# Attention scores on chip laid out by blocks of 32 queries first, and their mirrored copies in longer pieces

## The chip, the core and the metric

The kernel runs on one core of a Trainium2 chip. The core has five engines that work side by side, each with its own in-order stream of instructions: TensorE (PE; its weight loads are a row of their own, PEld), VectorE (DVE), ScalarE (ACT), GpSimd (POOL) and SyncE (SP), which here only issues DMAs. Sixteen DMA engines move data between the main memory (HBM) and the on-chip memory (SBUF); TensorE writes its products to PSUM. The metric is the device time of one execution in microseconds (us). Lower is better.

## What is computed

Two stages. The first is a gated attention unit without softmax: for each of 8 batches the scores of all pairs of 2496 positions, a squared ReLU, a product with `v`, and a gate `u`. The second sends each of the 19968 rows through one of 8 small networks, chosen by a hash of its token.

```python
scores = scale * np.matmul(z, z.transpose(0, 2, 1))     # z: 8 x 2496 x 64
attn = np.maximum(scores, 0.0) ** 2
out = np.matmul(attn, v)                                # v: 8 x 2496 x 256
x = (u * out).reshape(B * S, D)
...
expert_idx = token_ids * 2654435761 % 8
for e in range(8):
    mask = expert_idx == e
    out[mask] = np.maximum(x[mask] @ w1[e], 0.0) @ w2[e]   # 256 -> 1024 -> 256
```

All data is 32-bit floating point. Since queries and keys are both `z`, the scores of a batch are a symmetric matrix.

## The kernel before

**Tiling of the attention.** The 2496 positions of a batch are two halves of 1248. A query group `g` (0 to 4) takes the same 256 positions of both halves (the last group 224), a key step `s` (0 to 4) likewise. So a batch has 25 steps of (g, s), in the order `STEPS`; all 8 batches make 200. A tile `a` of one step holds 512 keys by 512 queries: 128 partitions, two tiles `j` of 128 keys, key half `h`, 8 blocks `m` of 32 queries (7 in the last group), query half `q`, and 32 queries `r` in a block. Before the change `a` is ordered `[j, h, m, q, r]` along a partition.

**Scores and their mirror.** Steps with `s >= g` are computed by `score`: four products on TensorE into PSUM (tag `mm`, four buffers), a ReLU by ScalarE for each (L244), then squares: on ScalarE (L250, L252), and for the step with `s == g` one half on VectorE (L248). When `s > g`, `mirror` transposes the tile on VectorE in 32 x 32 blocks (L274), and `keep` stores it to HBM through SP's queue in four DMAs (L283), or in seven for the last group of keys in the last batch (L287). Steps with `s < g` are not computed: `recall` reads the mirrored tile back by a DMA that ScalarE issues (L291). So 15 of 25 steps are computed, 10 are stored and read back: 80 tiles in all. The tiles `a` have four buffers, the mirrors two.

**One step.** `sums` makes four combinations `t` of the quarters of `a` on VectorE (L263 to L266); `attend` then makes seven products in place of eight (a scheme of Strassen's kind) of two matmuls each (L312) into the four PSUM tiles `acc`. The trace counts each 32-bit matmul as two MATMUL records, so a step has 28. Products 1, 2 and 3 read quarters of `a` as their moving operand, the others read `t`. After the last step of a group, `join` copies and adds the seven products (L323 to L331) and so frees the banks of `acc` for the next group; its second instruction is L325.

**What sets the order.** The order in each engine's stream is the order of the program text (`tc.manual_schedule()`). In loop pass `i` it is: `sums` for step `i + 2` (with its `score` ahead of it), `recall` for step `i + 3`, `keep` for the mirror made in the pass before, loads and transposes of the next batch's `z` (`load_z` L160, `turn_z` L173, `copy_z` L178), `attend` for step `i`, `join` if it ends a group, `mirror` for step `i + 2`, loads and sums of `v`. After these come the work on finished groups (`gate`, `put` L352, `fetch` L360 and L208, `multiply` L377, the scatter `sort` on GpSimd), the routing `places` during batch 0, and the preparation of the expert weights (`prepare`, L656 to L672). SP issues nearly all loads and stores in this order and waits in it for whatever each DMA needs; so does VectorE.

The second stage (L886 on) begins when the last group has been joined. It is run by the same kind of products (L928, L959, L982, L993) and reads weights and rows by DMA.

Of the kernel before, what the change touches and what calls it, by code (L numbers as in the profile page):

```python
# [10 lines left out]
F32 = mybir.dt.float32  # L11
# [13 lines left out]
def kernel(  # L25
# [10 lines left out]
    nc = tc.nc  # L36
# [4 lines left out]
    E, _, F = moe_w1.shape  # L41
# [3 lines left out]
    P = 128  # L45
    L = 32
# [18 lines left out]
    W = 256  # L65
# [10 lines left out]
    QB = P // L  # L76

    def in_turn(b, g):
        return (b, g) != (B - 1, NG - 1)
# [17 lines left out]
    def pool(name, bufs, **kw):  # L97
# [9 lines left out]
    mpool, zpool = (closing["z and mirrors"].enter_context(tc.tile_pool(name=name, bufs=2, side="right")) for name in ("mpool", "zpool"))  # L107
    vpool, apool, opool, xpool = (
        attention.enter_context(tc.tile_pool(name=name, bufs=bufs))
        for name, bufs in (("vpool", 6), ("apool", 3), ("opool", 2), ("xpool", 1)))  # L110

    def blocks(g):
        return min(W, HS - g * W) // L

    mirrored = {(b, g, s): nc.dram_tensor(f"scores_{b}_{g}_{s}", (2 * W, blocks(s) * 2 * L), F32)
                for b in range(B) for s in range(NG) for g in range(s)}


# [24 lines left out]
    def keys(s, j):  # L145
        return P if (s, j) != (NT - 1, 1) else KL

    def queries(g):
        return min(W, HS - g * W)
# [61 lines left out]
    def flat(ps):  # L211
        return ps[:].rearrange("p t q c -> p (t q c)")

    def score(b, g, s):

        w, nb = queries(g), blocks(g)
        a = apool.tile([P, 2, 2, W // L, 2, L], F32, name="a", bufs=4)
        made = []  # L220
        for j in range(2):
            for h in range(2):
                z_h = zT[b][ts(h, K), :]
                q_h = z_h[:, 0:S].rearrange("k (q c) -> k q c", q=2)[:, :, ds(g * W, w)]
                ps = mm_ps.tile([P, 2, 2, P], F32, name="s_ps", tag="mm")
                if w == W:
                    to, at = ps.rearrange("p t q c -> p q t c"), q_h.rearrange("k q (t c) -> k q t c", t=2)
                else:
                    to, at = flat(ps)[:, 0:2 * w].rearrange("p (q c) -> p q c", q=2), q_h
                nc.tensor.matmul(to, z_h[:, ds(h * HS + s * W + j * P, P)], at, start=True, stop=True)  # L230
                made.append((j, h, ps))
        for j, h, ps in made:

            if w == W:
                parts = ((a[:, j, h].rearrange("p (i t) q r -> p (t q) i r", t=2), ps[:].rearrange("p t q (i r) -> p (t q) i r", r=L)),)
            else:
                at = flat(ps)[:, 0:2 * w].rearrange("p (q m r) -> p q m r", q=2, r=L)
                if in_turn(b, g):
                    parts = [(a[:, j, h].rearrange("p (i t) q r -> p t q i r", t=2)[:, t, :, 0:keys(g, t) // L],
                              at[:, :, ds(t * QB, keys(g, t) // L)]) for t in range(2)]  # L240
                else:
                    parts = ((a[:, j, h, 0:nb].rearrange("p m q r -> p q m r"), at),)
            for to, at in parts:
                nc.scalar.activation(to, at, AF.Relu, scale=1.0 / S)  # L244
            if h:
                o = a[:, j].rearrange("p h m q r -> p h (m q r)")[:, :, 0:2 * w]
                if j and s == g:
                    nc.vector.tensor_mul(o, o, o)  # L248
                elif j:
                    nc.scalar.activation(o, o, AF.Square)  # L250
        o = a[:, 0].rearrange("p h m q r -> p h (m q r)")[:, :, 0:2 * w]
        nc.scalar.activation(o, o, AF.Square)  # L252
        return a

    def halves(a, g, h, q):
        return a[:, :, h, 0:blocks(g), q]

    def sums(g, a):

        t = apool.tile([P, 4, 2, W], F32, name="t")  # L260
        y11, y12, y21, y22 = (halves(a, g, h, q) for h in range(2) for q in range(2))
        t1, t2, t3, t4 = (t[:, i, :, 0:queries(g)].rearrange("p j (m r) -> p j m r", r=L) for i in range(4))
        nc.vector.tensor_sub(t1, y12, y11)  # L263
        nc.vector.tensor_sub(t3, y22, y12)  # L264
        nc.vector.tensor_sub(t2, y22, t1)  # L265
        nc.vector.tensor_sub(t4, t2, y21)  # L266
        return a, t

    def mirror(a):

        m = mpool.tile([P, 2 * W // L, 2, 2, L], F32, name="mirror")
        for j in range(2):
            for h in range(2):
                nc.vector.transpose(m[:, :, j, h].rearrange("p (n i) k -> p i n k", i=QB),  # L274
                                    a[:, j, h].rearrange("p (i t) q r -> p i (t q) r", t=2))
        return m

    def keep(b, g, s, m):
        to = mirrored[b, g, s].rearrange("(m r) e -> r m e", r=L)
        for i in range(QB):  # L280
            if in_turn(b, s):
                n = 2 * L * len(range(2 * i, min(2 * i + 2, blocks(s))))
                nc.sync.dma_start(out=to[:, :, ds(i * 4 * L, n)], in_=m[ts(i, L)].rearrange("p n j h k -> p n (j h k)")[:, :, 0:n])  # L283
            else:
                for j in range(2):
                    if j * QB + i < blocks(s):
                        nc.sync.dma_start(out=to[:, :, ts(j * QB + i, 2 * L)], in_=m[ts(i, L), :, j].rearrange("p n h k -> p n (h k)"))  # L287

    def recall(b, g, s):
        a = apool.tile([P, 2, 2, W // L, 2, L], F32, name="a", bufs=4)  # L290
        nc.scalar.dma_start(  # L291
            out=a[:].rearrange("p j h m q k -> p (j h) (m q k)")[:, :, 0:blocks(g) * 2 * L],
            in_=mirrored[b, s, g].rearrange("(n p) e -> p n e", p=P))
        return a


# [2 lines left out]
    def attend(b, g, s, at, acc, first, last):  # L299
        w = queries(g)  # L300
        a, t = at
        vs, c = v_sb[b, s], vc_sb[b, s]
        x11, x12, x21, x22 = (vs[:, h, :, ts(i, P)] for i in range(2) for h in range(2))
        s1, s2, s4 = (c[:, i] for i in range(3))
        y11, y12, y21, y22 = (halves(a, g, h, q) for h in range(2) for q in range(2))
        t1, t2, t3, t4 = (t[:, i, :, 0:w] for i in range(4))
        for i, (m, x, y) in enumerate(((1, x11, y11), (2, x12, y21), (5, s1, t1), (3, s4, y22), (6, s2, t2), (7, x21, t3), (4, x22, t4))):
            k, half = BANK[m]
            for j in range(2):
                n = keys(s, j)  # L310

                nc.tensor.matmul(acc[k][:, half, 0:w], x[0:n, j, :], y[0:n, j], start=(first and j == 0 and half == 0),  # L312
                                 stop=(last and j == 1), skip_group_check=True)
# [446 lines left out]
    def recall_early(i):  # L760
        if i < len(steps) and steps[i][2] < steps[i][1]:
            scores[i] = recall(*steps[i])

    def prepare_scores(i):
        if i < len(steps):
            b, g, s = steps[i]
            if s >= g and i >= AHEAD:
                scores[i] = score(b, g, s)
            ready[i] = sums(g, scores[i])
            return scores.pop(i)  # L770
# [6 lines left out]
    def prepare_mirror(i, a):  # L777
        if i < len(steps) and steps[i][2] > steps[i][1]:
            mirrors.append((*steps[i], mirror(a)))


    for i in range(AHEAD):
        scores[i] = score(*steps[i])
# [5 lines left out]
    for i, (b, g, s) in enumerate(steps):  # L789
        pos = i % NT  # L790
        to_keep, mirrors = mirrors, []
        a = prepare_scores(i + AHEAD)
        recall_early(i + AHEAD + 1)
        for m in to_keep:
            keep(*m)
# [58 lines left out]
        for part, after in enumerate((0, 4, 5, 7)):  # L854
            k, due = divmod(i - PREP - after, PERIOD)
# [170 lines left out]
    for i in range(NBIG + 1):  # L1026
        parts = {}
# [55 lines left out]
```

## Time and profile before

| | |
|---|---|
| median of 3 runs | 2508.42 us (2508.22 to 2512.26) |
| the profiled execution | 2508.14 us, its span 2506.4 us |
| ACT busy | 724.2 us, 29% |
| DMA packets | 583400 (284236 under 512 B, 525213 under 2 KB) |
| DMA queue of SP (q1) | 363.19 MB, 53.9% of 16 engines' span |
| DMA queue of ScalarE (q10) | 97.86 MB, 12.1% |
| store of a mirrored tile, 276 DMAs of 256 KB | median 5.0 us from issue to landing |
| read-back, 48 of 1024 KB and 32 of 896 KB | median 5.8 and 7.4 us |

The span is the time from the first to the last instruction of the program. A busy time is the time in which an engine had an instruction running. "Landing" is when a DMA's completion was signalled. A wait is idle time of an engine, put down to what ended it; the name behind `<-` is the engine, tile and line, or the DMA. The attention takes the first 1470 us of the span.

### The profile page before, as it was taken

How to read it: one execution, taken by the hardware profiler on the slowest of the kernel's cores; microseconds unless marked ns; L12 is line 12 of the kernel's file. 1: busy time of each engine (PE TensorE's matmuls, PEld its weight loads, DVE VectorE, ACT ScalarE, POOL GpSimd, SP SyncE). 2: the span in 40 equal slices, each digit the busy share in tenths (PEclk: the TensorE clock that was granted, in tenths of full speed). 3: DMA queues.
4: the chain of work that ended last, by engine and by line, in shares of the span. 5: the costliest groups of instructions: out<-in, count | busy, mean ns of one | idle time of the engine just before them, and what ended most of it. 6: DMA issues, size and time to landing. Idle time of an engine off the chain costs nothing.

```text
span 2506.4 us, 37323 instructions
## 1 busy us (share of the span) xinstructions
PE 2474.0 (99%) x13751; PEld 2110.9 (84%) x13751; DVE 1715.3 (68%) x3346; ACT 724.2 (29%) x1259; POOL 547.2 (22%) x532
## 2 busy tenths in 40 slices
PE   8999999999999999999999999999999999999998
PEld 6787786787787787787787889999999999999998
DVE  7799758768768778777677656655665565556554
ACT  4314313314324224223233112222222222222221
POOL 0000243233313331332233211111111111121212
PEclk9999999999999999999999999999999999999999
DMA  8766798798788798897897886767685767667672
GB/s 148 181 177 163 212 275 239 192 274 223 222 238 223 207 254 209 234 256 187 244 250 198 237 259 211 275 215 218 202 260 189 261 194 253 210 227 234 212 247 75
DMA packets 583400, 550.67 MB, mean 220 GB/s; under 512 B 284236, under 2 KB 525213, under 8 KB 571184
## 3 DMA queue, kind: packets, MB, share of 16 engines
q1 hardware_dynamic: 492720, 363.19, 53.9%
q10 hardware_dynamic: 63168, 97.86, 12.1%
q0 software_dynamic: 27328, 87.23, 9.8%
q8 instruction: 108, 1.77, 0.3%
q14 instruction: 76, 0.62, 0.1%
HBM read 371.36 MB, written 173.24 MB: 217 GB/s over the span
## 4 chain that ended last, share of the span: by engine, by line
PE 91%; DMA 4%; DVE 3%; issue 1%; ACT 0%; SPq 0%; POOL 0%; ACTq 0%; POOLq 0%; DVEq 0%
PE acc L312 42%; PE o_ps L959 17%; PE h_ps L928 17%; PE s_ps L230 9%; PE h_ps L982 3%; PE o_ps L993 3%; DMA a<-scores 2%; DMA u_sb<-in_u_dram 1%; DMA zn<-in_z_dram 0%; DMA scores<-mirror 0%; DVE t L263 0%; DVE t L264 0%; DVE x_row L377 0%; DVE t L265 0%; DVE t L266 0%
## 5 line engine op out<-in xcount | busy, mean ns | idle before, releaser
L244 ACT ACTIVATE a<-s_ps 128x512 f32<-128x512 f32 (+2 forms) x508 | 248.4, 578 | 751.8 <-PE s_ps L230 690.0
L312 PEld LDWEIGHTS acc<-a,v_sb 128*128 128x128 f32 (+1 forms) x1600 | 295.2, 191 | 128.7 <-issue 45.5
L312 PE MATMUL acc<-t,vc 128*128 128x256 f32 (+3 forms) x1600 | 403.1, 374 | 0.0
L312 PE MATMUL acc<-a,v_sb 128*128 128x256 f32 (+3 forms) x1600 | 385.8, 384 | 7.8 <-DVE o L325 7.7
L312 PE MATMUL acc<-t,v_sb 128*128 128x256 f32 (+3 forms) x1600 | 369.7, 373 | 0.0
L399 POOL DMA_INDIRECT x_slots<-x_row,row x160 | 185.9, 1162 | 819.6 <-DVE x_row L377 667.5
L312 PEld LDWEIGHTS acc<-t,vc 128*128 128x128 f32 (+1 forms) x1600 | 304.0, 190 | 34.5
L312 PEld LDWEIGHTS acc<-t,v_sb 128*128 128x128 f32 (+1 forms) x1600 | 303.4, 190 | 33.6
L263 DVE TENSOR_TENSOR t<-a 128x512 f32<-128x512 f32 (+1 forms) x200 | 134.2, 671 | 234.2 <-ACT a L252 164.6
L928 PE MATMUL h_ps<-xs,w 128*128 128x256 f32 (+1 forms) x1248 | 288.5, 361 | 0.0
L959 PEld LDWEIGHTS o_ps<-w,h 128*128 128x128 f32 x2272 | 275.8, 192 | 7.8 <-DVE ro L892 1.1
L880 POOL DMA_INDIRECT out_dram<-o_sb,idx x142 | 143.5, 1011 | 629.7 <-issue 406.5
L959 PE MATMUL o_ps<-w,h 128*128 128x128 f32 x2272 | 279.3, 275 | 0.6 <-DVE ro L892 0.6
L230 PE MATMUL s_ps<-zT 64*128 64x512 f32 (+1 forms) x960 | 244.7, 619 | 15.2 <-DVE zT L173 8.3
L935 ACT ACTIVATE h<-h 128x512 f32<-128x512 f32 (+1 forms) x234 | 138.5, 592 | 355.6 <-DVE h L898 143.5
L928 PEld LDWEIGHTS h_ps<-xs,w 128*128 128x128 f32 x1248 | 208.6, 191 | 16.5
L928 PE MATMUL h_ps<-xT,w 128*128 128x256 f32 (+1 forms) x936 | 215.0, 362 | 2.9 <-DVE h L898 2.9
L959 PEld LDWEIGHTS o_ps<-w,hs 128*128 128x128 f32 x1704 | 206.9, 192 | 4.9
L959 PE MATMUL o_ps<-w,hs 128*128 128x128 f32 x1704 | 209.3, 275 | 0.0
L274 DVE STREAM_TRANSPOSE mirror<-a 128x512 f32<-128x512 f32 x320 | 198.3, 676 | 5.4 <-DMA scores<-mirror 5.4
L312 PE MATMUL acc<-a,vc 128*128 128x256 f32 (+3 forms) x800 | 201.1, 373 | 0.0
L626 POOL DMA_INDIRECT slot_tokens<-token,addr x160 | 171.1, 1069 | 65.7 <-issue 48.4
(176 smaller groups left out, 2631.9 us busy)
## 6 DMA issues: line engine op xcount, KB each, us to landing
w<-w_blocks SPq DMA_DIRECT2D x78, 1792.0 KB, 11.0
scores<-mirror SPq DMA_DIRECT2D x276, 256.0 KB, 5.0
a<-scores ACTq DMA_DIRECT2D x48, 1024.0 KB, 5.8
a<-scores ACTq DMA_DIRECT2D x32, 896.0 KB, 7.4
w_blocks<-w POOLq DMA_DIRECT2D x16, 1792.0 KB, 7.6
w1s<-in_moe_w_dram SPq DMA_DIRECT2D x21, 1024.0 KB, 9.6
w2s<-in_moe_w_dram SPq DMA_DIRECT2D x21, 1024.0 KB, 15.6
u_sb<-in_u_dram SPq DMA_DIRECT2D x72, 256.0 KB, 5.4
```

What stands on the lines that cost most here:

```text
L230: nc.tensor.matmul(to, z_h[:, ds(h * HS + s * W + j * P, P)], at, start=True, stop=True)
L244: nc.scalar.activation(to, at, AF.Relu, scale=1.0 / S)
L263: nc.vector.tensor_sub(t1, y12, y11)
L274: nc.vector.transpose(m[:, :, j, h].rearrange("p (n i) k -> p i n k", i=QB), a[:, j, h].rearrange("p (i t) q r -> p i (t q) r", t=2))
L312: nc.tensor.matmul(acc[k][:, half, 0:w], x[0:n, j, :], y[0:n, j], start=(first and j == 0 and half == 0), stop=(last and j == 1), skip_gro ...
L399: st = nc.gpsimd.indirect_dma_start(out=x_dram[:, :], out_offset=bass.IndirectOffsetOnAxis(ap=row[0:m, c:c + 1], axis=0), in_=x_sb[0:m, q, ...
L626: st = nc.gpsimd.indirect_dma_start(out=slot_dram[:, None], out_offset=bass.IndirectOffsetOnAxis(ap=addr[0:n, to:to + 1], axis=0), in_=tok ...
L880: st = nc.gpsimd.indirect_dma_start(out=out[:], out_offset=bass.IndirectOffsetOnAxis(ap=idx[:, col:col + 1], axis=0), in_=o, in_offset=Non ...
L928: nc.tensor.matmul(ps[:, r], w1[j][:, k, ts(f + r, P)], y, start=first and r == 0, stop=True, skip_group_check=True)
L935: lambda o, i, k, ps=None: nc.scalar.activation(o, o if ps is None else ps, AF.Relu))
L959: nc.tensor.matmul(ps[:, t], x[:, f, ts(t, P)], w2_block(w2[j], k)[:, f], start=first and t == 0 and f == 0, stop=f == FQ - 1, skip_group_ ...
L982: nc.tensor.matmul(ps[:, i, :], w1[j][:, c, ts(f + i, P)], x[:, 0, c, 0:P], start=(c == 0), stop=(c == DP - 1))
```

## The change

The tile `a` is ordered `[m, j, h, q, r]`: the block of 32 queries comes first, and all that belongs to one block lies together (1024 B in a partition). The mirrored tile in HBM becomes 128 rows (a row of the mirrored tile's partitions) of 8192 B (7168 B for the last group), and is stored in pieces of 2048 B where it was 512 B. The read-back is one contiguous piece for each partition, where it was four of 2048 B. To write the new order, the ReLU of a full-width step is split in two (`t` = 0 and 1, 256 queries each), and each of the four transposes of a mirror in two. The squares and `halves` address the new order. The number of DMAs and the places where they are issued stay as they were.

```diff
     def blocks(g):
         return min(W, HS - g * W) // L
-    mirrored = {(b, g, s): nc.dram_tensor(f"scores_{b}_{g}_{s}", (2 * W, blocks(s) * 2 * L), F32)
+    mirrored = {(b, g, s): nc.dram_tensor(f"scores_{b}_{g}_{s}", (P, blocks(s) * 8 * L), F32)
                 for b in range(B) for s in range(NG) for g in range(s)}
...
         w, nb = queries(g), blocks(g)
-        a = apool.tile([P, 2, 2, W // L, 2, L], F32, name="a", bufs=4)
+        a = apool.tile([P, W // L, 2, 2, 2, L], F32, name="a", bufs=4)
         made = []
         for j in range(2):
             for h in range(2):
...
         for j, h, ps in made:
             if w == W:
-                parts = ((a[:, j, h].rearrange("p (i t) q r -> p (t q) i r", t=2), ps[:].rearrange("p t q (i r) -> p (t q) i r", r=L)),)
+                parts = [(a[:, :, j, h].rearrange("p (i t) q r -> p t q i r", t=2)[:, t], ps[:, t].rearrange("p q (i r) -> p q i r", r=L))
+                         for t in range(2)]
             else:
                 at = flat(ps)[:, 0:2 * w].rearrange("p (q m r) -> p q m r", q=2, r=L)
                 if in_turn(b, g):
-                    parts = [(a[:, j, h].rearrange("p (i t) q r -> p t q i r", t=2)[:, t, :, 0:keys(g, t) // L],
+                    parts = [(a[:, :, j, h].rearrange("p (i t) q r -> p t q i r", t=2)[:, t, :, 0:keys(g, t) // L],
                               at[:, :, ds(t * QB, keys(g, t) // L)]) for t in range(2)]
                 else:
-                    parts = ((a[:, j, h, 0:nb].rearrange("p m q r -> p q m r"), at),)
+                    parts = ((a[:, 0:nb, j, h].rearrange("p m q r -> p q m r"), at),)
             for to, at in parts:
                 nc.scalar.activation(to, at, AF.Relu, scale=1.0 / S)
             if h:
-                o = a[:, j].rearrange("p h m q r -> p h (m q r)")[:, :, 0:2 * w]
+                o = a[:, 0:nb, j].rearrange("p m h q r -> p m (h q r)")
                 if j and s == g:
                     nc.vector.tensor_mul(o, o, o)
                 elif j:
                     nc.scalar.activation(o, o, AF.Square)
-        o = a[:, 0].rearrange("p h m q r -> p h (m q r)")[:, :, 0:2 * w]
+        o = a[:, 0:nb, 0].rearrange("p m h q r -> p m (h q r)")
         nc.scalar.activation(o, o, AF.Square)
         return a
     def halves(a, g, h, q):
-        return a[:, :, h, 0:blocks(g), q]
+        return a[:, 0:blocks(g), :, h, q].rearrange("p m j r -> p j m r")
     def sums(g, a):
...
     def mirror(a):
-        m = mpool.tile([P, 2 * W // L, 2, 2, L], F32, name="mirror")
+        m = mpool.tile([P, QB, 2, 2, 2, 2, L], F32, name="mirror")
         for j in range(2):
             for h in range(2):
-                nc.vector.transpose(m[:, :, j, h].rearrange("p (n i) k -> p i n k", i=QB),
-                                    a[:, j, h].rearrange("p (i t) q r -> p i (t q) r", t=2))
+                for t in range(2):
+                    nc.vector.transpose(m[:, :, j, t, :, h], a[:, :, j, h].rearrange("p (i t) q r -> p t i q r", t=2)[:, t])
         return m
     def keep(b, g, s, m):
-        to = mirrored[b, g, s].rearrange("(m r) e -> r m e", r=L)
-        for i in range(QB):
+        to = mirrored[b, g, s].rearrange("(i r) e -> r i e", r=L)
+        for k in range(QB):
+            at = m[ts(k, L)].rearrange("p i j t q h r -> p i (j t q h r)")
             if in_turn(b, s):
-                n = 2 * L * len(range(2 * i, min(2 * i + 2, blocks(s))))
-                nc.sync.dma_start(out=to[:, :, ds(i * 4 * L, n)], in_=m[ts(i, L)].rearrange("p n j h k -> p n (j h k)")[:, :, 0:n])
+                n = 8 * L * len(range(2 * k, min(2 * k + 2, blocks(s))))
+                nc.sync.dma_start(out=to[:, :, ds(k * 16 * L, n)], in_=at[:, :, 0:n])
             else:
                 for j in range(2):
-                    if j * QB + i < blocks(s):
-                        nc.sync.dma_start(out=to[:, :, ts(j * QB + i, 2 * L)], in_=m[ts(i, L), :, j].rearrange("p n h k -> p n (h k)"))
+                    if j * QB + k < blocks(s):
+                        nc.sync.dma_start(out=to[:, :, ts(j * QB + k, 8 * L)], in_=at[:, :, ts(j, 8 * L)])
     def recall(b, g, s):
-        a = apool.tile([P, 2, 2, W // L, 2, L], F32, name="a", bufs=4)
-        nc.scalar.dma_start(
-            out=a[:].rearrange("p j h m q k -> p (j h) (m q k)")[:, :, 0:blocks(g) * 2 * L],
-            in_=mirrored[b, s, g].rearrange("(n p) e -> p n e", p=P))
+        a = apool.tile([P, W // L, 2, 2, 2, L], F32, name="a", bufs=4)
+        nc.scalar.dma_start(out=a[:].rearrange("p m j h q k -> p (m j h q k)")[:, 0:blocks(g) * 8 * L], in_=mirrored[b, s, g][:, :])
         return a
```

## The prediction

> **What bounds the kernel now.** I read the page's busy times first, then the list of who TensorE waited for, then the timeline around its longest waits, then windows for clock and DMA share, and last the groups kept apart by shape. All is summed against the profiled execution: span 2506.4 us, its own time 2508.14 us, 0.3 us from the median 2508.42.
>
> ```profile
> PE 2474.0 (99%) x13751; PEld 2110.9 (84%) x13751; DVE 1715.3 (68%) x3346; ACT 724.2 (29%) x1259; POOL 547.2 (22%) x532
> ```
> TensorE is the bound: 2474 of 2506 us. No other engine can gain more than what TensorE idles, plus matmuls that ran slowly. Its idle time, by what ended it:
> ```profile
> PE s_ps L230 <- DVE zT L173: 8.3, 2, 7.1
> PE acc L312 <- DVE o L325: 7.7, 6, 2.1
> PE s_ps L230 <- DMA zT<-zT: 5.2, 1, 5.2
> PE h_ps L928 <- DVE h L898: 2.9, 2, 2.5
> PE s_ps L230 <- ACT a L244: 1.7, 2, 1.0
> PE o_ps L959 <- DVE ro L892: 0.6, 1, 0.6
> ```
> (columns: us in total, times, longest.) These are 26.4 us, of which 7.1 is the first load of z. The rest is where the change can help. Two timelines show what is behind it. At the boundary between query groups 3 and 4 of batch 3:
> ```profile
> 700.43 1.19 SPq L283 DMA_DIRECT2D scores<-mirror  x2
> ...
> 704.70 0.92 SPq L160 DMA_DIRECT2D zn<-in_z_dram  x2
> ...
> 713.39 0.94 DVE L173 STREAM_TRANSPOSE zT<-zn 64x736 f32<-64x736 f32 x1 [5.17 <-DMA zn<-in_z_dram]
> ...
> 715.88 1.62 DVE L377 TENSOR_TENSOR x_row<-x_row,u_sb 128x256 f32<-128x256 f32 x4 [1.55 <-DMA u_sb<-in_u_dram]
> ...
> 720.90 0.41 DVE L325 TENSOR_TENSOR o<-r,acc 128x256 f32<-128x256 f32 x1
> ...
> 721.36 1.78 PE L312 MATMUL acc<-a,v_sb 128*128 128x224 f32 x8 [1.72 <-DVE o L325]
> ```
> VectorE stood 5.2 us for z and 1.6 us for u, both queued on SP behind the stores of a mirrored tile. From there it worked without a pause and came 1.7 us late to the join (L325) that frees the first bank of acc. In the chain of waits at the start of batch 2 the mirrored tiles stand themselves:
> ```profile
> 357.75 11.52 DMA scores<-mirror
> ...
> 369.49 6.97 DMA a<-scores
> ...
> 383.60 4.56 DMA zT<-zT
> ```
> A store took 11.5 us to land, the read-back that needs it 7.0, and the copy of z 4.6 behind both; TensorE stood 5.17 us at 388.30. The windows around it, and one after the boundary in batch 5:
> ```profile
> 380.00:388.20 8.20, 3.12 (x13) 2.01 (x12) 8.00 (x16) 1.03 (x3) 2.21 (x2) 0.86 1.00 293
> 388.30:396.00 7.70, 7.70 (x16) 4.38 (x17) 7.56 (x19) 3.69 (x5) 5.07 (x7) 0.50 0.96 325
> ...
> 1082.00:1085.50 3.50, 3.48 (x10) 3.16 (x11) 3.29 (x8) 0.39 (x1) 2.59 (x4) 0.53 0.93 228
> ```
> (the last three columns are granted clock, DMA share, GB/s.) The DMA engines were full, and after the stall TensorE ran at half its clock: matmuls started 427 ns apart instead of 216.
>
> [...] 512 B took 39 ns on average (13 GB/s for an engine), 2048 B 97 to 101, 14336 B 540 in the median. [...]
>
> **The change part by part.** The groups that price it:
> ```profile
> L244 ACT ACTIVATE a<-s_ps 128x512 f32<-128x512 f32 x448 | 231.8, 602 | 712.3 <-PE s_ps L230 655.4 <-DMA x_row<-x 39.4 <-DMA zn<-in_z_dram 17.5
> L274 DVE STREAM_TRANSPOSE mirror<-a 128x512 f32<-128x512 f32 x320 | 198.3, 676 | 5.4 <-DMA scores<-mirror 5.4
> L343 DVE STREAM_TRANSPOSE x_sb<-o 128x256 f32<-128x256 f32 x124 | 43.3, 404 | 6.6 <-DMA x<-x_sb 6.6
> L244 ACT ACTIVATE a<-s_ps 128x256 f32<-128x256 f32 x28 | 11.4, 408 | 34.6 <-PE s_ps L230 29.6 <-DVE t L266 4.9
> ```
> *Relu.* 448 of 128x512 become 896 of 128x256. In a row four of the first span 2.06 us, so one starts every (2.06 - 0.60)/3 = 0.49 us; six of 256 and 192 span 1.60, one every 0.24. Taking 0.27 for 256: 7 x 0.27 + 0.41 = 2.28 us, +0.22 per scored tile. Two isolated ones would be 4 x (2 x 408 - 602) = +0.86 us; that is the upper end. ScalarE is at 29%, so only its lateness counts.
>
> *Mirror.* 320 transposes become 640. Four of 512 span 2.48 us, four of 256 span 1.42 (a start every 0.34): 7 x 0.34 + 0.40 = 2.78, +0.30 us for each of 80 tiles, 24 us on VectorE, which idles 791. Upper end, isolated: 4 x (2 x 404 - 676) = +0.53.
>
> *Squares, sums.* As many elements, runs of 32 or 128 at a larger stride; sums already read runs of 32. Cost 0.
>
> *Matmuls on a.* The three products that take a itself (12 of 28 MATMUL records of a step) read runs of 128 B at 1024 B stride instead of 256. Before, strided a and contiguous t both start every 216 ns, so I take 0; a nanosecond on 2400 records would be 2.4 us.
>
> *Waits.* The instruction order of the new program has 374 more waits of TensorE on its own semaphore, before score matmuls (the previous product in that PSUM buffer), all long satisfied. In the old trace 15 second matmuls of a score pair carry such an extra wait, and the typical one starts 6 to 7 ns behind its partner like the others; 37 of L928 start at 216 ns as without. Cost 0, at most 374 x 7 ns = 2.6 us.
>
> *DMAs.* As many instructions on SP and ACT, in the same order. A stored tile of 1 MB goes from 2048 packets x 39 ns / 16 engines = 5.0 us to 512 x 97 / 16 = 3.1; a read-back from 512 x 101 / 16 = 3.2 to 128 x 310 / 16 = 2.5 (8192 B estimated from 14336 B in 540 ns). With the smaller tiles of the last group that is about 190 us of all engines' time, and the DMA share over 700 to 1470 us falls from 0.85 to about 0.72.
>
> *What this is worth on TensorE's path.* (a) Boundaries 3 to 4 in batches 1, 3, 5, 6: waits of 1.05, 1.72, 1.89, 0.72 us, plus 9 records that each ran about 184 ns over in batch 5: 7.0 us. z and u land some 2 us sooner there (1.9 of store, 0.7 of read ahead of them, less 0.3 of later mirror), more than each wait: I take 80%, -5.6. (b) Batch 2: 1.04 + 5.17 idle, scores at half clock 2.3, nine records at +0.21: 10.4 us. From 320 to 370 us the engines have about two stores and six reads less to do by 2 x 1.9 + 6 x 0.65 = 7.7 us; 70%, -7. (c) The start of the second stage waits 2.5 + 0.3 us for a VectorE that had stood 9.2 us for u and 1.2 for a read-back, then runs about 1.6 us of half clock: half of 4.4, -2.2. Behind a stall that goes, the next thing late is the join itself: sums and the join end within 0.1 us of TensorE's need at five boundaries from group 2 to 3, so nothing more follows.
>
> *What is lost.* At those five, and one at 0.04, the relus' +0.22 shows: 1.2. In batch 0 VectorE works without a pause from 144 us to the join of group 3 (routing): the wait of 2.14 grows by 0.22 + 0.30, 0.5. The start, two scores deep in ScalarE: 0.5. The first boundary of batch 1 (0.14 us to spare): 0.3. Together +2.5.
>
> Sum: 2508.1 - 14.8 + 2.5 = **2496 us**; with every gain 2488, with a third of it 2506.
>
> **The rivals.**
> *Hidden anyway.* The DMAs shorten but z and u still wait behind SP's in-order queue for the mirror or for buffers; stalls stay, or similar ones appear elsewhere, since where transfers collide is chance. Half the stalls of (b) go at best. 2508 + 2.5 - 2 = 2508.5. For it: SP's waits on mirrors and read-backs are many. Against it: the DMA share of 1.00 where the longest stall is.
>
> *Slower: the halves are late at the group boundaries.* If relus and transposes cost their isolated durations, VectorE is 0.86 + 0.53 = 1.39 us later at each join. From the ends of L325 and of the last matmul before it, 18 boundaries have less to spare; their shortfalls sum to 21 us, less 5 for batch 2: 2524. It decides from about 0.7 us of lateness per boundary. Against it: the overlap of both kinds in a row is in the timeline.
>
> *Slower: a matmul pays for the wider stride.* From 5 ns a record, 12 us, it outweighs most of the gain: at 10 ns 2520. Nothing in the trace speaks for it.
>
> *More than forecast.* All stalls named go: 2487.
>
> **How the numbers follow.** Forecast 0.52, hidden 0.24, late halves 0.12, stride 0.05, more 0.07. About 0.2%, 5 us, can be told from no change: 2503.4 to 2513.4. Of the forecast 0.48 lies below 2503.4, with 0.07: faster 0.55. Hidden gives 0.18 to same and 0.06 to slower; with 0.04 of the forecast same is 0.22, slower 0.23. The forecast's own range is 2488 to 2506; to leave out only the two slower cases and the tails, 2486 to 2513.
>
> **What would show it.** Right: stores landing in under 4 us instead of 5.0, read-backs in under 5 instead of 5.8 and 7.4; q1's share from 53.9% to about 48%; the wait of s_ps for zT gone and that of acc for L325 under 4 us; VectorE's busy time up by about 25 us, ScalarE's by 30 to 60. Wrong: 128x256 relus or transposes that do not overlap, more waits of acc for L325, matmuls on a above 216 ns apart, or a new stall of several us at another batch's start.

## The result

| | before | after |
|---|---|---|
| median (20 runs each) | 2508.1 us (2502.94 to 2512.26) | 2503.74 us (2498.41 to 2509.26) |
| ratio | | 0.9982, 95% interval 0.9976 to 0.9989 |
| the profiled execution | 2508.14 us, span 2506.4 | 2500.07 us, span 2498.0 |

The change makes the kernel 4.4 us faster, where 12 were forecast. The time lies inside the range; the size of the gain does not fit. The profiled execution of after happens to lie 3.7 us below its median, so the pair of traces differs by 8.1 us: nearly twice what the change is worth. A second profile of after (e4 below) is used beside it.

### The profile page after: what moved, and what is told of

Its sections match the earlier page's. It is cut to its first block, busy times and chain, and to the rows that moved or that the text cites. A ratio compares the mean times of both kernels' runs of the same rounds, so it can differ in the third digit from the quotient of the medians.

```text
span 2498.0 us, 38465 instructions
## 1 busy us (share of the span) xinstructions
PE 2471.3 (99%) x13751; PEld 2112.1 (85%) x13751; DVE 1734.8 (69%) x3666; ACT 752.4 (30%) x1707; POOL 551.0 (22%) x532
## 3 DMA queue, kind: packets, MB, share of 16 engines
q1 hardware_dynamic: 365232, 363.19, 51.6%
## 4 chain that ended last, share of the span: by engine, by line
PE 94%; DVE 2%; DMA 2%; issue 1%; ACT 0%; SPq 0%; POOL 0%; ACTq 0%; POOLq 0%; DVEq 0%
PE acc L313 45%; PE o_ps L960 17%; PE h_ps L929 17%; PE s_ps L231 9%; PE h_ps L983 3%; PE o_ps L994 3%; DMA x_row<-x 1%; ACT a L246 0%; DMA a<-scores 0%; DMA u_sb<-in_u_dram 0%; DVE t L265 0%; DVE t L267 0%; DVE t L266 0%; DVE zT L174 0%; DMA zT<-zT 0%
## 5 line engine op out<-in xcount | busy, mean ns | idle before, releaser
L246 ACT ACTIVATE a<-s_ps 128x256 f32<-128x256 f32 x956 | 276.8, 412 | 723.6 <-PE s_ps L231 610.2
L400 POOL DMA_INDIRECT x_slots<-x_row,row x160 | 193.1, 1207 | 805.5 <-DVE x_row L378 704.1
L277 DVE STREAM_TRANSPOSE mirror<-a 128x256 f32<-128x256 f32 x640 | 217.5, 406 | 3.5 <-DMA scores<-mirror 3.5
```

The lines of the kernel that those rows point to most:

```text
L277: nc.vector.transpose(m[:, :, j, t, :, h], a[:, :, j, h].rearrange("p (i t) q r -> p t i q r", t=2)[:, t])
L400: st = nc.gpsimd.indirect_dma_start(out=x_dram[:, :], out_offset=bass.IndirectOffsetOnAxis(ap=row[0:m, c:c + 1], axis=0), in_=x_sb[0:m, q, ...
```

## The profile after

The page's busy times of after:
```profile
PE 2471.3 (99%) x13751; PEld 2112.1 (85%) x13751; DVE 1734.8 (69%) x3666; ACT 752.4 (30%) x1707; POOL 551.0 (22%) x532
```
VectorE has 19.5 us more work and ScalarE 28 us (about 25 and 30 to 60 were forecast); TensorE is the bound still. The list of who TensorE waited for (us, times, longest), first of after, then of its second profile:
```profile
PE s_ps L231 <- DVE zT L174: 8.2, 2, 7.1
PE acc L313 <- DVE o L326: 4.4, 5, 2.6
PE h_ps L929 <- DVE h L899: 2.5, 1, 2.5
PE s_ps L231 <- DMA zT<-zT: 2.2, 1, 2.2
PE acc L313 <- DVE t L268: 1.0, 1, 1.0
```
```profile
PE acc L313 <- DVE o L326: 6.6, 7, 2.6
PE acc L313 <- DVE t L268: 4.0, 2, 2.1
PE h_ps L929 <- DVE h L898: 2.5, 1, 2.5
PE s_ps L231 <- DMA zT<-zT: 2.0, 1, 2.0
```
In the first, the stalls at the boundaries of groups 3 and 4 in batches 3, 5 and 6 are gone (0.12 us left) and the one of batch 2 has shrunk from 5.2 to 2.2. In the second, the same boundaries wait 1.84, 2.12, 1.67 and 0.47 us in batches 1, 3, 5 and 6: 6.1 us, more than the 5.4 of before. So the stalls were not removed for good: they come and go between executions. The reason is in a list that the prediction did not print, what SP waited for with a DMA to issue. Its largest rows for read-backs, of before and of after:
```profile
SPq L283 <- DMA a<-scores: 373.4, 37, 17.4
...
SPq L352 <- DMA a<-scores: 80.3, 9, 15.3
...
SPq L160 <- DMA a<-scores: 50.4, 9, 12.1
```
```profile
SPq L286 <- DMA a<-scores: 289.1, 29, 21.1
...
SPq L361 <- DMA a<-scores: 51.3, 4, 13.6
SPq L161 <- DMA a<-scores: 51.2, 11, 10.1
```
SP stood for read-backs that *ScalarE* issues: 577 us in all rows of this kind before, 483 after (507 in the second profile), up to 21 us at a time. L161, L209, L353 and L361 are the loads of z, of u, and the store and load of the gated rows; none of them reads what a read-back writes. The trace tells why they wait: its record of a DMA names the semaphore that the landing increments. In after the 1,091 DMAs of SP and the 168 of ScalarE have eight of them in turn (numbers 100 and 102 to 108, 157 or 158 DMAs each), and 1,218 of the 1,259 come behind a wait on their own semaphore, which the preceding DMA on it, the eighth before it, increments when it lands. Around 363 us of after, in the order of the turn, with the times of issue in us (the rows are of SP, but for the marked one; ScalarE's loads of v in between are left out):
```
359.80  z load   L161   increments semaphore 103
363.38                  ScalarE: read-back L294   increments semaphore 104
360.76  z load   L161   increments semaphore 105
362.13  x_row    L361   increments semaphore 107
363.23  u load   L209   increments semaphore 102
373.36  u load   L209   waits for semaphore 104, then increments it
373.77  copy z   L179   increments semaphore 105
```
The read-back has its place ahead of the second z load, but stands in ScalarE's own stream and was issued at 363.4 us, after it. SP's second load of u had to wait for it to land: the last increment of semaphore 104 by the read-back came at 373.34 us, and the load was issued at 373.36. In this stretch, SP's waits and the chain of what ended last (start, us, what) of after show
```profile
SPq L209 <- DMA a<-scores: 9.3, 1, 9.3
```
```profile
362.13 13.88 DMA x_row<-x
...
376.08 5.43 DMA u_sb<-in_u_dram
...
381.88 1.03 DVE x_row L378 x3
382.91 3.78 DMA zT<-zT
386.69 0.81 issue
387.50 2.62 PE s_ps L231 x6
```
From 364.1 to 373.4 us SP, in order, issued nothing: the z copy behind these u loads came too late, and TensorE stood 2.24 us at the start of batch 2, then ran at half its clock (0.50 granted, matmuls 427 ns apart). The last transpose of z had ended at 376.6 us, 6.3 us before its copy was issued. Not all of that is the one wait: SP stood for other landings (of v, z and gated rows) behind it, and VectorE itself stood 8.1 us for the data of the same read-back. In the trace of before, the like was read as slow stores and read-backs.

## The experiments

**Theories.** 1: stores read from 32 partitions stay slow whatever their pieces (packets of 2048 B took 132 ns, median 147, not 97), so that the transfers got only some 75 us of 16 engines' time shorter, not 190. 2: the split relus and transposes eat the gain. 3: DRAM or other traffic sets the packets' time. 4: the transfers are hidden by now. 5: the prediction's estimate, 39 ns for a packet of 512 B wherever it is read. 6, formed after the first eight runs: SP's standing for read-backs. Times are medians; ratios are to the kernel before on the same chip.

**e1: the split alone, in the kernel before.**
```diff
-  parts = ((a[:, j, h]... "p (t q) i r", ps "p (t q) i r"),)
+  parts = [(a[:, j, h]... [:, t], ps[:, t]...) for t in range(2)]
-  nc.vector.transpose(m[:, :, j, h]..., a[:, j, h]...)
+  for t in range(2): nc.vector.transpose(m...[:, t], a...[:, t])
```


> The kernel before, with only the relus of a score tile and the transposes of a mirror split in two; shapes of all DMAs as before. Theory 1 (the split costs 2.5 us and the stores gained less than forecast): 2510.5 us, ratio 1.001, TensorE idles 28 to 30 us instead of 26.4, with waits of 0.2 us at the five boundaries from group 2 to 3, about 1 us at the first boundary of batch 1 and 2.6 us at that of batch 0. Theory 2 (the split eats the gain): 2515 us or more, ratio 1.003 or above, TensorE idles over 33 us. In both VectorE is busy 19 us more and ScalarE 28 us more than before, as in the changed kernel.

2511.81 against 2507.95 us, ratio 1.0018 (1.0011 to 1.0024): +3.9 us, between the two. The waits are as forecast, 2.64 us at batch 0's boundary where it was 2.14, 1.12 in batch 1 and 0.2 each at five boundaries. What was left out is that behind 2.64 us eight matmul records ran at half clock, some 1.5 us; behind 2.14 they had not. (The length of the wait does not settle that, as the last section shows.)

**e4: the changed kernel again.**

> The changed kernel once more, for a second profile and as the base of the others. All theories: 2503.7 us, ratio 0.998. If the stalls at the starts of batch 2 (2.2 us) and of the second stage (2.5 us) and that of batch 0 (2.6 us) are set by the order of the work, they are there again within 0.3 us; if they are chance of colliding transfers, they differ by 1 us or more, or stand elsewhere.

2503.73 us, 0.9981 (0.9973 to 0.9989). The stalls of batch 0, of batch 2 and of the second stage are there again within 0.3 us; those of the boundaries differ, as shown above.

**e7: the change without the split.** The score tile is `[i, j, h, t, q, r]`, where the block `m` was `(i t)`, so t and q merge again for one relu and one transpose; all DMAs are those of the changed kernel.
```diff
-  parts = [(a[...][:, t], ps[:, t]) for t in range(2)]
+  parts = ((a "p i j h t q r"[:, :, j, h] as "p (t q) i r", ps "p (t q) i r"),)
```


> The changed kernel with its stores and read-backs, but with the score tile laid out so that relus and transposes are one instruction each as in the kernel before (the last query group apart). If the split costs what the run of the split alone showed (3.9 us): 2499 to 2500.5 us, the waits of 0.2 us at the boundaries from group 2 to 3 gone. If the split's cost there was chance of the stalls: 2503 to 2504 us.

2498.86 against 2506.65 us, 0.9967 (0.9954 to 0.998). So the longer pieces are worth -8 us and the split costs 4; together they are the change. Theory 2 is a small part of it: the split costs 1.4 us more than the 2.5 forecast, of 7.6 that are missing. SP stood for read-backs 587 us here, no less than before, and yet the kernel is 8 us faster: the total of that list does not measure the loss, it matters which loads stand behind a wait.

**e2, e5, e6: from which partitions the stores read.** e2 stores all 128 partitions at a time, e5 64, both in the changed kernel; e6 does what e2 does in the kernel before. In all three the mirrored blocks land in permuted places, so products with read-back tiles use other blocks and the output is not that of the function; sizes and counts are kept (e5 stores 4 MB more, in four more DMAs).
```diff
-  at = m[ts(k, L)]...                  # 32 partitions, 4 block rows
+  at = m[:, k]...                      # e2: 128 partitions, 1 block row
+  at = m[ts(k // 2, 2 * L), ts(k % 2, 2)]...   # e5: 64 partitions, 2 block rows
```


> The changed kernel, but each of the four stores of a mirrored tile takes one block row of all 128 partitions instead of all four block rows of 32 partitions: as many DMAs, as many packets of 2048 B, the same rows of 2048 B in DRAM. Theory 1 (a store that reads 32 partitions is held back where it reads them): the packets of 2048 B take 85 to 105 ns in the mean instead of 132, the DMA share from 700 to 1470 us falls from 0.81 to 0.77, and the time to 2499 to 2502 us, ratio to the kernel before 0.9965. Theory 3 (what the transfers take is decided in DRAM or by other traffic): packets of 130 ns still, time 2503.7 as the changed kernel. Theory 4 (the transfers are hidden by now): packets quicker, time 2503 to 2505 all the same.

> The changed kernel with stores of 64 partitions (0 to 63, then 64 to 127), two block rows a store, 128 packets of 2048 B as before. The mirrored blocks land in permuted places, as in the run that stored 128 partitions at a time; all sizes are the same. Theory 1 in its sharp form[...]: packets of 127 to 140 ns, 2502 to 2506 us. If the number of partitions counts instead: 100 to 112 ns, 2494 to 2498 us.

> The kernel before, its pieces of 512 B and its unsplit relus and transposes kept, but each store takes pieces from all 128 partitions; the mirrored blocks land in permuted places. Theory 1[...]: packets of 512 B take 24 to 30 ns instead of 39, 106 us of 16 engines' time less, 2492 to 2498 us. Theory 5 (the prediction's reading: a packet of 512 B costs 39 ns for its fixed part, wherever it is read): 39 ns and 2507 to 2509 us.

| | us | ratio | stores' packets |
|---|---|---|---|
| e2 | 2490.22 | 0.9929 (0.9915 to 0.9943) | 2048 B in 91 ns |
| e5 | 2489.89 | 0.9934 (0.9921 to 0.9946) | 4096 B in 250 ns |
| e6 | 2486.31 | 0.9922 (0.9908 to 0.9935) | 512 B in 29 ns |

For the packets theory 1 is right, and theories 3 and 5 are not: 91 ns from 128 partitions, and 512 B, whose 39 ns the prediction took for the price of any packet of that size, in 29. (In e5 two neighbouring pieces merged into one of 4096 B.) For the time it is wrong. The queue of SP, of after and of e5:
```profile
q1 hardware_dynamic: 365232, 363.19, 51.6%
```
```profile
q1 hardware_dynamic: 346352, 367.38, 51.3%
```
e5 kept the engines as long with its packets as after did, and yet ran as fast as e2 (47.5%). What all three share is another list, SP's waits of e5:
```profile
SPq L733 <- PE h_ps L928: 351.9, 34, 21.0
SPq L286 <- DVE mirror L277: 338.7, 49, 14.6
SPq L286 <- DVE vc L200: 159.9, 18, 20.7
SPq L352 <- DVE x_sb L343: 137.2, 14, 17.0
```
SP waits for its work to be made; the read-backs have fallen to 15, 31 and 27 us. A read-back stands where it stood in ScalarE's stream, but takes its place in the rotation later: 18 or 19 places behind the last store that it waits for, in the median, where it was 11 in the kernels before and after. That is the author's count in the order of the programs, not shown by a trace.

**e9, e10, e11: read-backs out of the rotation.** One line, in the changed kernel, in the kernel before, and in e7's:
```diff
-  nc.scalar.dma_start(out=a[...], in_=mirrored[b, s, g]...)
+  nc.gpsimd.dma_start(out=a[...], in_=mirrored[b, s, g]...)
```


> The changed kernel, its stores still from 32 partitions, with one edit: the read-backs are issued by GpSimd instead of ScalarE, so that they no longer take a place in the rotation of eight completion semaphores that the DMAs of SP and ScalarE share. Theory 6 (SP, which issues a DMA only when the eighth one before it in that rotation has landed, stood 483 to 507 us for read-backs in the changed kernel, and z, u and the stores stood behind it): SP's waits for read-backs fall below 50 us, the packets of stores stay at 130 ns or above, TensorE idles 16 to 18 us, and 2488 to 2493 us, ratio 0.993. Theory 1 (the time of the stores' packets decides): 2502 to 2505 us. GpSimd issuing late, behind its other work, would show as VectorE waiting for read-backs and over 2505 us.

> The kernel before with the same one edit; pieces of 512 B, read-backs in pieces of 2048 B, nothing split. Theory 6: 2485 to 2490 us, ratio 0.992, with packets of 512 B at 38 to 41 ns as before, and so faster than the changed kernel without any of its change. Theory 1: 2506 to 2509 us.

> The same one edit on the kernel with the changed stores and read-backs and unsplit relus and transposes. Theory 6: 2485 to 2489 us, within 1.5 us of the kernel before with the edit, so that the larger pieces are worth nothing once SP no longer stands for read-backs. If the larger pieces are still worth something then: 4 us or more below it. Theory 1: 2499.

2493.57 us, 0.9955 (0.9942 to 0.9969); 2495.46, 0.9959 (0.9945 to 0.9972); 2488.87, 0.9937 (0.9923 to 0.9951), against 2506.39. SP's waits for read-backs are nil in all three, the stores' packets nearly as slow as before (128, 37 and 130 ns), and all are some 11 us or more faster: theory 6, not theory 1. The edit also takes the read-backs out of ScalarE's stream and queue; e12 to e14, which leave them there, answer that. e9 and e10 miss their numbers, and the 6.6 us between e10 and e11 are against what was expected. In their place SP now stood 313 to 322 us for loads of v, which ScalarE issues too, and e10 kept a stall at the start of batch 2. Its timeline:
```profile
383.96 3.73 PE L230 MATMUL s_ps<-zT 64*128 64x512 f32 x6 [1.94 <-DMA zT<-zT]
387.62 3.56 PE L312 MATMUL acc<-a,v_sb 128*128 128x256 f32 x8
```
Six scores in 3.73 us and eight records in 3.56 are half clock (eight take 1.7 where they start 216 ns apart); in e11 the stall was 1.43 us and no half clock followed. This and the same at batch 0 (2.33 against 2.14 us) make up 5.5 of the 6.6: e11 is ahead by 1.7 us more behind the one place, and by 3.8 behind the other. Most of that is half clock, which need not be the longer pieces' doing.

**e12, e13, e14: half of the stores issued by ScalarE.** e12 in the changed kernel, e13 in e7's, e14 in the kernel before.
```diff
-  for k in range(QB):
-      nc.sync.dma_start(out=..., in_=...)
+  for k in (0, 2, 1, 3):
+      (nc.scalar if k > 1 else nc.sync).dma_start(out=..., in_=...)
```


> The changed kernel with the stores of partitions 64 to 127 issued by ScalarE instead of SP, read-backs on ScalarE as before. In the order of its instructions a read-back takes its place in the rotation later (19 places behind the last store that it needs, in the median, as in the quick kernels; 11 in the changed kernel). Theory 6: SP's waits for read-backs below 100 us, 2488 to 2494 us, unless ScalarE's relus wait for its stores (then more). Theory 1: 2498 to 2503, as packets of both halves are in flight together. If neither: 2503.7 or above.

> Stores of partitions 64 to 127 issued by ScalarE, pieces of 2048 B and 8192 B, relus and transposes unsplit. Theory 6 with a split worth 3.9 us: 2486 to 2488 us, ratio 0.992, TensorE idles under 15 us (7.1 and 1.1 at the start, 2.1 at the end of batch 0's group 3, 2.5 at the start of the second stage).

> The kernel before with the one edit that stores of partitions 64 to 127 are issued by ScalarE; pieces of 512 B and 2048 B. If larger pieces are worth nothing once SP does not stand for read-backs: within 1 us of e13 (2486 to 2489 us). If they are worth what e10 against e11 showed: 2492 to 2494 us, with a stall at the start of batch 2 of over 1.5 us and matmuls at half clock behind it.

e12: 2490.6 us against 2506.39, 0.994 (0.9926 to 0.9953). e13: 2486.13 (2485.67 to 2487.59) against 2504.75, 0.9923 (0.991 to 0.9937). e14: 2486.2 (2484.79 to 2488.22), 0.9923 (0.9909 to 0.9936). Of e14 the list of TensorE's waits, SP's waits, and the chain around the start of batch 2:
```profile
PE s_ps L230 <- DVE zT L173: 7.2, 1, 7.2
PE h_ps L929 <- DVE h L899: 2.5, 1, 2.5
PE acc L313 <- DVE o L326: 2.1, 1, 2.1
PE s_ps L230 <- ACT a L244: 1.2, 1, 1.2
PE o_ps L960 <- DVE ro L893: 0.6, 1, 0.6
```
```profile
SPq L284 <- DVE mirror L274: 373.0, 53, 13.8
...
SPq L353 <- DMA a<-scores: 41.2, 11, 6.4
```
```profile
379.86 6.24 PE acc L313 x28
386.10 1.92 PE s_ps L230 x8
388.01 4.08 PE acc L313 x18
```
All stalls inside the attention but one are gone, and the chain is TensorE alone; SP stood 79 us for read-backs in all (40 in e12, 51 in e13). These three alone would not rule out theory 1, for their packets got quicker too: the stores that ScalarE issued took 99, 100 and 30 ns in the mean, those of SP 124, 131 and 38. e9 to e11 and e5, with packets nearly as slow as ever, do. e13 and e14 differ in the longer pieces, and in the time by 0.1 us, within the spread of either: with SP free, the change's pieces are worth nothing that can be told. The kernel before with this one edit is faster than the changed kernel by 0.0058 in the ratio, some 14 us, and no kernel that computes the whole was faster than these two.

**Two misses.** e3 puts e2's wide stores right, block by block, with e7's layout: each store's target is then 4 by 32 rows of 2048 B. e8 cuts each store in four.
```diff
+  out=to[i].rearrange("r (k e) -> k r e", k=QB), in_=m[:, i]...       # e3
+  for i, k in ((i, k) for i in range(QB) for k in (0, 2, 1, 3)): ...  # e8
```


> The wide stores of the run before, and a layout of the score tile (blocks i, then key half j, h, query half t, q) in which relus and transposes are one instruction each as in the kernel before; only the last query group keeps the order of the changed kernel. Theory 1: the split's 2.5 us come back too, 2497 to 2500 us, ratio 0.9955; the waits of 0.2 us at the boundaries from group 2 to 3 are gone. Theory 2 (the split eats most of the gain): 2494 or less. Theory 4: 2501 to 2503. A product that pays for three strides in its moving operand would show as records over 216 ns apart and 5 us or more.

> The changed kernel with each store cut into four (one block row of 32 partitions, 32 packets of 2048 B), in the order of partitions 0, 64, 32, 96[...]; 16 stores a tile instead of 4. [...] If stores are served one after the other: 132 ns, and 2503 to 2508 us, since SP issues 12 more stores a tile.

e3: 2776.38 us, 1.1064 (1.1048 to 1.1079). Of 1088 us with store packets in flight, 557 had exactly four. The target's outermost count is 4 as well; that this count is the cause was not shown. VectorE's waits of e3:
```profile
DVE mirror L299 <- DMA scores<-mirror: 152.7, 26, 12.8
```
Matmuls with three strides in the moving operand still started 216 ns apart. e8: 2584.74 us, 1.0316 (1.03 to 1.0331), with packets of 119 ns; 16 stores a tile fill the rotation twice over, and SP stood 386 us for read-backs and VectorE 65 us for stores.

## Where the prediction was right and where it failed

- *The step that failed* is the one headed "What this is worth on TensorE's path". It put the lateness of z and u down to the time of the store and the reads ahead of them ("z and u land some 2 us sooner there"). e5, e9 and e11 show that those loads come in time (but for 1.1 and 1.4 us at the start of batch 2 in e9 and e11) with packets nearly as slow as ever, once SP does not stand for read-backs. The change left 483 of 577 us of that standing. The rival "hidden anyway" had the wait behind SP's in-order queue, though not the shared semaphores that cause it, and named SP's waits on read-backs as what spoke for it; it got 0.24, because the DMA share of 1.00 at the longest stall was taken for the cause.
- *The sum, term by term.* TensorE runs the same 13,751 matmul records in the same order in all these kernels, so the difference of the start times of a record tells where time was won or lost against before (us; one profile each):

| | forecast | after | after, second profile | e1: split alone | e7: pieces alone | e14: old pieces, two issuers |
|---|---|---|---|---|---|---|
| (a) | -5.6 | -6.1 | +0.7 | -4.7 | -7.2 | -7.5 |
| (b) | -7 | -5.3 | -5.6 | -1.4 | -2.4 | -12.0 |
| (c) | -2.2 | -2.2 | -2.6 | +0.2 | -0.9 | -0.9 |
| all else ("What is lost") | +2.5 | +5.3 | +4.7 | +8.7 | +1.5 | -1.3 |

e14 wins more at (a) and (b) than the forecast, and has none of the change: the lateness was not that of the pieces.
- *(a)*: in the first profile 4.2 us less waiting in the four batches and 1.7 less half clock, which is the forecast; in the second 0.7 more waiting, and nine records at half clock in batch 3 in place of batch 5. It is not a gain that every execution has, and e1 had most of it without longer pieces. *(b)* came nearest to what was forecast, in both profiles: the longest wait fell by 3 us and the one of 1.04 before it went, while the half clock behind the longest stayed; e7 with the same transfers won less than half of it. *(c)* has the right number by luck. The wait stayed, 2.5 us in both profiles; what went is 1.6 us of half clock behind it, which was also missing in e1, behind a wait of 3.2, and is there in e7 and e14, behind 2.5. No DMA is late at that place. The timeline of after shows VectorE with four sums of the hidden layer ahead of the three additions that free TensorE's bank:
```profile
1473.31 0.68 DVE L940 TENSOR_TENSOR hs<-h 128x512 f32<-128x512 f32 x1
1474.02 0.69 DVE L941 TENSOR_TENSOR hs<-hs,h 128x512 f32<-128x512 f32 x1
1474.63 0.69 DVE L942 TENSOR_TENSOR h<-h 128x512 f32<-128x512 f32 x1
...
1475.23 0.69 DVE L943 TENSOR_TENSOR hs<-h,hs 128x512 f32<-128x512 f32 x1
1475.83 0.68 DVE L893 TENSOR_TENSOR r<-r,h_ps 128x512 f32<-128x512 f32 x1
1476.62 0.69 DVE L898 TENSOR_TENSOR h<-r,h_ps 128x512 f32<-128x512 f32 x1
1477.41 0.69 DVE L899 TENSOR_TENSOR h<-h,h_ps 128x512 f32<-128x512 f32 x1
...
1478.15 1.13 PE L929 MATMUL h_ps<-xT,w 128*128 128x256 f32 x4 [2.50 <-DVE h L899]
```
- *The DMA sum*, 190 us of 16 engines' time: some 75 (the packets of SP's and ScalarE's queues took 1656 us before and 1581 after). A packet of 2048 B was priced at 97 ns from transfers over 128 partitions, and took 132 from 32. Read-backs of 8192 B took 375 in the mean, 309 in the median, as estimated. The share of q1 fell to 51.6%, not 48. The page of after has no landing times; in e7, whose transfers are the same, a store lands in 4.3 us, not under 4, and a read-back in 4.9 and 6.1.
- *What is lost*, +2.5, was sized too small: 3.9 in e1's time, and some 5 in the two profiles of after. The five boundaries and batch 0's wait came as forecast; the first boundary of batch 1 grew by 1.1 instead of 0.3, and the half clock behind batch 0's wait, 1.4 us (0.50 granted for 3.41 us in after), was not counted. (The relus' sum, 7 x 0.27 + 0.41, is 2.30, not 2.28; nothing hangs on it.)
- *Costed at nothing*, and rightly: the wider stride of the matmuls (216 ns apart still) and TensorE's 374 added waits (the second scores of a pair start 6 to 7 ns behind their partners, as before).

What stays open: why a read-back takes its place in the rotation early in one program and late in another; the order of the programs shows only that it does. What part of the -8 us of the longer pieces in e7 came from which transfer was not separated. And the table's rows move by several us between two executions of one kernel, so that they show where time went in these profiles, not what each place is worth on average.

## What to carry to other kernels

When a load is late, ask first what its issuing engine stood for. A full DMA and a slow transfer next to it prove little when the queue behind it is in order, and here DMAs of two engines wait for each other through a shared set of eight semaphores: the list of SP's waits had 577 us on one name. Before a change to the data's layout, try the edit that only moves the issue: here a change of who issues half of the stores was worth 18 us, and the layout on top of it nothing. And take two profiles before counting stalls of a microsecond: at the same three boundaries the same kernel had 0.1 us of them in one and 4.3 in the next.

## What the runs showed of the hardware

- Stores that read 32 partitions moved 16 x 2048 B in 147 ns (median), 223 GB/s, and no faster in pieces of 512 B (16 x 512 in 41, 200 GB/s). From 64 partitions they were hardly quicker in the engine time of their packets: 61 us for each MB in e5 (4860 in all), against 64 from 32 partitions in after (4765) and 44 from 128 in e2 (3299). What holds them back was not shown. Nor is it the price of every packet from 32 partitions: the stores that ScalarE issued beside SP's in e12 read as many, and their packets of 2048 B took 99 ns in the mean, 84 in the median.
- Whether half clock follows a stall of 2 to 3 us cannot be told from the stall's length. It followed stalls of 1.89 us (before, batch 5), 1.94 (e10, batch 2), 2.16 (e7, batch 0) and 2.5 (before, second stage); in the trace of before the granted clock was 0.50 for 3.41 us behind the 1.89 and again behind the 2.5. It did not follow 2.14 (before, batch 0; 1.00 granted), 2.5 (after, second stage; 1.00 granted), 2.65 (e2, batch 0) and 3.2 (e1, second stage). The half clock can cost more than the stall: in e10, some 3 us behind 1.94.
